# Pooled attention product on 64x64 tiles inside the value product, and a TensorE order that weighs changes of tile mode

## The chip, the core and the metric

The kernel runs on one core of a Trainium2 chip. Its engines work side by side, each on its own queue in program order: PE (TensorE, matrix products into PSUM), DVE (VectorE), ACT (ScalarE), POOL (GpSimd), and SP, which here only issues transfers (DMA). The metric is the device time of one execution in microseconds (us), as the median of several runs. PSUM has eight banks here: two for attention (`att`), one each for the gate and value products, and four for the output products (`o0` to `o3`).

## What is computed

The reference is attention followed by a gated layer. Attention is the sum of a local part (each query sees keys at most 3 positions away) and a pooled part (queries, keys and values averaged over groups of 4, full softmax over 144 groups, the result repeated 4 times):

```
q_d, k_d, v_d = means of q, k, v over groups of 4 positions       # S 576 -> 144
out_up    = repeat(softmax(q_d k_d^T / sqrt(D)) v_d, 4)
out_local = softmax(mask(|i-j| < 4, q k^T / sqrt(D))) v           # both softmaxes divide by sum + 1e-9
x   = (out_up + out_local), heads side by side                    # 4608 x 512
out = (sigmoid(x w_gate) * (x w_val)) w_out                       # 512 -> 1536 -> 512
```

There are 8 batches and 8 heads, with 64 numbers a head.

## The kernel before

**Units and chunks.** Attention is cut into 32 units (u = 0 to 31), each two heads of one batch. The gated layer ("MoE") is cut into 9 chunks of 512 tokens. Units 0 to 7 (`early`) feed chunks 0 and 1, units 8 to 31 (`later`) the rest. Chunks 0 and 1 are plain products with 12 + 12 + 12 groups (`pg` gate, `pv` value, `po` output, 12 matmuls of 512 columns each); from chunk 2 on there are 42 pairs of `bank` products (256 columns, line L832) and `obank` output products (L971) in a seven-product scheme.

**A unit's steps.** In the names of the code, with the engine: `s` (PE, local scores, 20 products on 64x64 tiles, the four corners of the array taken in turn), `st`/`mx`/`sm` (DVE), `sb`/`tm` (POOL), `ex` (ACT); `tt0`, `tt1` (PE, transposes into `at`, L446), `tc0`, `tc1` (ACT, copies out of PSUM); `sd` (PE, pooled scores, tiles of 64 rows), `dm` (DVE), `de` (ACT), `dn` (POOL, the softmax weights `ad`); `dt` (PE, six transposes into `adt`), `dc` (ACT copy); `va`, `vB` (POOL, pooled values `vdblk`: the two heads' 64x64 blocks on the diagonal of a 128x128 tile, zeros beside them); `do` (PE, tile `od`: three full-array products of 144 columns, L418); `oc` (ACT, `od` scaled by `sxb` and repeated four times); `x` (PE, local value product, 20 products on 64x64 tiles of 58 columns, L423, into two banks, one for each half of the queries); `xa0`, `xa1` (DVE, L595 and L1276: bank times `sxb` plus `od`, into the chunk's input). `fp32` products leave two records each in the trace.

**What sets the order.** Every step is an `op` with an engine, a planned duration, predecessors and the banks it needs. `order()` walks through planned time: for each free engine it takes the ready op with the earliest due time `late`, where `GOALS` and `PACE` set the due times. The result is a fixed order on each engine. On PE, whatever is ready among the next `PACE['ahead']` MoE products competes with the attention steps. The function `bank` inside `later` always takes one of the two `att` banks.

**Weights and the first chunk.** Until about 160 us the weights are loaded and split into two fp16 halves (L225 to L255, ACT and DVE), while units 0 to 7 and chunk 0 run. `pg0` needs the attention outputs of units 0 to 3 (`xl`, L1293, on POOL or DVE) and the first low half of w_gate (`lo`, L255).

**Transfers.** SP issues all of them in order: `load_qk`, `load_qkd`, `load_vd`, `vload`, and the weight pieces of the pairs (`fetch`, L814). An issue that waits holds all later ones.

Of the kernel before, what the change touches and what calls it, by code (L numbers as in the profile page):

```python
# [22 lines left out]
PACE = {'a0': -6.52, 'a': 6.04, 's0': 25.787, 'sp': 8.115, 'e': 2.605, 's': -0.706, 'sd': 0.86, 'tt': 13.445, 'dt': 12.18, 'do': 15.987, 'x': 16.17, 'b3': -1.06, 'b4': -2.399, 'b5': -4.037, 'b6': -0.29, 'b7': 3.324, 'extra': -0.177, 'ahead': 36}  # L23
GOALS = {'x0': 33.486, 'x0s': 7.26, 'pv': 73.942, 'pvs': 6.2, 'x1': 117.291, 'x1s': 28.832, 'po': 221.56, 'pos': 26.01, 'c1': 150.991}
INTURN = ("s", "sd", "tt0_", "tt1_", "dn", "dt", "vB", "do", "x")
# [10 lines left out]
HALF = NJ * R  # L36
TURNS = ((0, 3), (3, NJ))
# [38 lines left out]
def attention_moe(ctx, tc, qk, qkd, v, vd, wg, wv, wo, mask, out):  # L76
# [73 lines left out]
    vdblk = [zeroed(nc.gpsimd, [P, NKC, P], F32, f"vdblk{i}") for i in range(2)]  # L150
    ad = zeroed(nc.gpsimd, [QM, 2, NKC, 2, WIN], F32, "ad")
    vring = cp.tile([P, NVR, NBLK * D], F32, tag="vring", name="vring")

    def vturn(b):
        pt = ps_a.tile([P, 512], F32, tag="att", name=uniq("mxt"))
        nc.tensor.transpose(pt[:1, :P], vm[b, "m1"], ident)
        return pt
# [6 lines left out]
    def spread(row, n, pt=None):  # L164

        if pt is None:
            pt = ps_a.tile([P, 512], F32, tag="att", name=uniq("mxt"))
        nc.tensor.matmul(pt[:, 256 : 256 + n], row.to_broadcast([n, P]), ident[:n, :n], start=True, stop=True)
        return pt[:, 256 : 256 + n]
# [136 lines left out]
    svb = cp.tile([P, B], F32, tag="svb", name="svb")  # L306
    sxb = cp.tile([P, B], F32, tag="sxb", name="sxb")
# [25 lines left out]
    def vscale(b, got):  # L333
        pow2(pvb[:, b : b + 1], got)
        inv_scaled(svb[:, b : b + 1], pvb[:, b : b + 1], 2.0 * VUP)
        nc.vector.tensor_scalar(out=sxb[:, b : b + 1], in0=svb[:, b : b + 1], scalar1=XUP / VUP, scalar2=None, op0=ALU.mult)
# [118 lines left out]

    def spans(r, segs):

        t0, t1 = r * HALF, min(r * HALF + HALF, S)
        return [(c, o + max(i, t0) - i, max(i, t0), min(i + w, t1)) for c, o, i, w in segs if max(i, t0) < min(i + w, t1)]

# [5 lines left out]
    SAME = dict(s="s{}", pb="pb{}", sd="sd{}", vB="vB{}", tt0="tt0_{}", tt1="tt1_{}", dn1="dn{}", dt="dt{}", do="do{}", x="x{}", xa1="xa1{}", qk="qk{}", tc0="tc0_{}", oc="oc{}", mx="mx1_{}", sm="sm{}")  # L466

    def later(u):
        b, hp = divmod(u, NPAIR)
        s = st[u] = {}  # L470
        AD, VDB = ad, vdblk[u % 2]
# [10 lines left out]
        def bank(name):  # L482
            return ps_a.tile([P, 512], F32, tag="att", name=name)
# [16 lines left out]
        def scores():  # L500
            s["s"] = [bank(f"s_{u}_{par}") for par in range(2)]
# [15 lines left out]
        def const(k, c):  # L517
            nc.scalar.activation(s[k], s[k], AF.Copy, scale=c, bias=EPS * c)
# [4 lines left out]
        def pooled():  # L523
            s["d"] = [bank(f"sd_{u}_{h}") for h in range(2)]
# [16 lines left out]
        def dnorm(qb):  # L541
            own(ad, u)
            nc.gpsimd.tensor_tensor(  # L543
                out=AD[:, qb].rearrange("p c h k -> p h c k")[:, :, :, :KC],
# [4 lines left out]
        def turn(i):  # L549
            s["a", i] = bank(f"at_{u}_{i}")  # L550
# [7 lines left out]
        def dturn():  # L558
            mine(ad, u)
            pt = s["ta"] = bank(f"adt_{u}")  # L560
            for c in range(NKC):
                for qb in range(2):
                    nc.tensor.transpose(pt[:, c * SD + qb * QM : c * SD + (qb + 1) * QM],  # L563
                                        AD[:, qb, c].rearrange("p h k -> p (h k)"), ident[:QM, :QM])

        def dturned():
            s["adt"] = wk.tile([P, NKC, SD], F32, tag="adt", name=f"adt16_{u}", bufs=1)
            nc.scalar.copy(s["adt"], s["ta"][:, : NKC * SD].rearrange("p (c q) -> p c q", c=NKC))

        def vB():  # L570
            own(VDB, u)
            for ps in HALVES:
                nc.gpsimd.tensor_tensor(out=VDB[ps, :, ps], in0=y()[ps, :, 0], in1=y()[ps, :, 1], op=ALU.add)
# [4 lines left out]
        def dout():  # L578
            mine(VDB, u)
            pt = s["do"] = bank(f"od_{u}")  # L580
            for c in range(NKC):
                product(pt[:, :SD], [VDB[:, c]], [s["adt"][:, c]], c == 0, c == NKC - 1)

        def dcopy():
            s["od"] = wk.tile([P, S], F32, tag="od", name=f"od_{u}")
            nc.scalar.activation(s["od"].rearrange("p (g f) -> p g f", f=4), s["do"][:, :SD].unsqueeze(2).to_broadcast([P, SD, 4]),
                                 AF.Copy, scale=sxb[:, b : b + 1])

        def local():
            s["x"] = [bank(f"x_{u}_{r}") for r in range(2)]  # L590
            each(value_pairs(u, s["at"], s["x"]))

        def both(r):
            for c, o, a, e in spans(r, segs_of_batch(b)):
                nc.vector.scalar_tensor_tensor(  # L595
                    out=xf(c)[:, hp, o : o + e - a], in0=s["x"][r][:, a - r * HALF : e - r * HALF],
                    scalar=sxb[:, b : b + 1], in1=s["od"][:, a:e], op0=ALU.mult, op1=ALU.add)
# [15 lines left out]
        add("vB", "P", 1.15, vB, ["va", old("do", 2)])  # L613
        add("s", "E", 0.75, scores, ["qk", old("tt1", 3), old("s", 1)], ["st0", "st1"])
# [1134 lines left out]
```

## Time and profile before

| | us |
|---|---|
| median of 3 runs (965.03 to 966.88) | 966.24 |
| the profiled execution | 966.05 |
| its span, first to last instruction | 964.3 |
| PE busy in the span | 936.0 |
| DVE, ACT, POOL busy | 720.5, 629.3, 378.3 |

The page's second part cuts the span into 40 slices of 24.1 us and gives each engine's busy share in tenths. The chain of the page's fourth part is walked back from the last instruction; 84% of it is PE. A row of the PE timeline gives the start, the length until the last product has drained, and the number of records; products overlap, so what a group costs is the distance from its start to the next group's start, not the length in the second column.

### The profile page before, as it was taken

What the parts mean: (1) busy time and instruction counts of PE and PEld (TensorE: products, weight loads), DVE (VectorE), ACT (ScalarE), POOL (GpSimd) and SP (SyncE); (2) the same over time, 40 slices, a digit from 0 to 9 for tenths busy, and PEclk for the clock granted to TensorE, in tenths of its full rate; (3) what the DMA queues carried; (4) which work ended last, traced back from release to release, by engine and by line L of the source; (5) the groups of instructions that cost most, each with busy time, mean ns of one, the idle gap of its engine ahead of it and who ended that gap; (6) DMA issues with size and microseconds to landing.
All of it is one profiled execution on the core that took longest, in us unless ns stands there. A gap on an engine that the chain in (4) does not pass through costs nothing.

```text
span 964.3 us, 23935 instructions
## 1 busy us (share of the span) xinstructions
PE 936.0 (97%) x9535; PEld 716.0 (74%) x9535; DVE 720.5 (75%) x1350; ACT 629.3 (65%) x1602; POOL 378.3 (39%) x387
## 2 busy tenths in 40 slices
PE   7788999999999999999999999999999999999998
PEld 5644544455548777788888888888888888888885
DVE  6899999578888679876868677787876686556644
ACT  6897775455446766677866776777667666555551
POOL 2264323356447655454555463256342133000000
PEclk9898999999999999999999999999999999999999
DMA  9899988264536887887878867786655555656631
GB/s 331 283 322 281 310 319 266 86 192 170 215 130 213 269 288 245 250 278 266 297 257 275 292 234 251 245 284 234 218 194 189 206 211 197 220 202 218 230 132 44
DMA packets 75360, 225.22 MB, mean 234 GB/s; under 512 B 18672, under 2 KB 29936, under 8 KB 74992
## 3 DMA queue, kind: packets, MB, share of 16 engines
q1 hardware_dynamic: 75248, 223.69, 68.2%
q8 instruction: 75, 1.23, 0.5%
q14 instruction: 37, 0.30, 0.1%
HBM read 196.66 MB, written 27.00 MB: 232 GB/s over the span
## 4 chain that ended last, share of the span: by engine, by line
PE 84%; DVE 6%; issue 1%; ACT 1%; DMA 1%; DVEq 0%; ACTq 0%
PE bank L832 39%; PE obank L971 16%; PE po L418 9%; PE pg L418 5%; PE pv L418 5%; PE x L423 2%; PE od L418 2%; PE s L423 2%; PE sd L423 2%; PE at L446 1%; PE adt L563 1%; DMA arena<-in_wg_dram 1%; DVE arena L712 1%; DVE arena L233 0%; DVE arena L229 0%
## 5 line engine op out<-in xcount | busy, mean ns | idle before, releaser
L832 PE MATMUL bank<-arena,wv 128*128 128x256 f16 x1764 | 220.2, 273 | 0.0
L832 PE MATMUL bank<-arena,wg 128*128 128x256 f16 x1764 | 220.1, 273 | 0.0
L832 PEld LDWEIGHTS <-wg 128*128 128x128 f16 x1764 | 171.3, 98 | 25.1 <-issue 0.8
L832 PEld LDWEIGHTS <-wv 128*128 128x128 f16 x1764 | 170.9, 98 | 25.4 <-issue 1.0
L971 PE MATMUL obank<-wo,spare 128*128 128x256 f16 x1071 | 147.3, 273 | 1.7 <-ACT obank L997 1.4
L971 PEld LDWEIGHTS <-spare 128*128 128x128 f16 x1071 | 103.3, 98 | 15.7 <-issue 3.3
L929 DVE SCALAR_TENSOR_TENSOR wo<-wg,wo 128x512 f16<-128x512 f32 (+1 forms) x136 | 93.2, 700 | 20.6 <-ACT wo L926 20.0
L715 POOL TENSOR_TENSOR wg<-wg 128x256 f32<-128x256 f32 x52 | 41.9, 806 | 127.5 <-DVE wo L929 110.8
L926 ACT ACTIVATE wo<-wg 128x512 f16<-128x512 f32 (+1 forms) x136 | 76.7, 577 | 17.8 <-DVE wg L862 9.3
L418 PE MATMUL po<-spare,wo 128*128 128x512 f16 x324 | 79.8, 380 | 0.0
L881 ACT COPY bank<-wv 128x256 f32<-128x256 f32 x84 | 31.7, 378 | 68.8 <-DVE wg L879 53.2
L879 DVE TENSOR_TENSOR wg<-bank,wv 128x512 f32<-128x512 f32 x63 | 43.4, 690 | 38.5 <-PE bank L832 34.5
L874 ACT COPY wv<-bank 128x512 f32<-128x512 f32 x84 | 48.8, 581 | 33.6 <-PE bank L832 32.8
L418 PE MATMUL pg<-arena,wg 128*128 128x512 f16 x288 | 67.7, 384 | 3.1 <-DVE wg L255 2.1
L418 PEld LDWEIGHTS <-wo 128*128 128x128 f16 x432 | 40.4, 98 | 39.7 <-issue 1.3
L418 PE MATMUL pv<-arena,wv 128*128 128x512 f16 x288 | 66.2, 379 | 0.0
L971 PE MATMUL obank<-wo,wv 128*128 128x256 f16 x357 | 58.4, 273 | 0.0
L543 POOL TENSOR_TENSOR ad<-e,sme 72x288 f32<-72x288 f32 x48 | 36.2, 770 | 53.3 <-DVE sme L521 25.0
L418 PEld LDWEIGHTS <-wg 128*128 128x128 f16 x288 | 28.0, 99 | 36.3 <-DVE wg L255 3.4
L712 POOL TENSOR_TENSOR arena<-arena 128x512 f16<-128x512 f32 (+1 forms) x27 | 29.0, 1077 | 61.7 <-ACT arena L708 61.7
L862 DVE SCALAR_TENSOR_TENSOR wg<-wg,bank 128x512 f32<-128x512 f32 x42 | 28.8, 685 | 30.3 <-PE bank L832 29.9
L418 PEld LDWEIGHTS <-wv 128*128 128x128 f16 x288 | 27.3, 98 | 31.6 <-issue 0.4
(200 smaller groups left out, 1838.4 us busy)
## 6 DMA issues: line engine op xcount, KB each, us to landing
wg<-wg SPq DMA_DIRECT2D x42, 896.0 KB, 4.7
wv<-wv SPq DMA_DIRECT2D x42, 896.0 KB, 4.7
spare<-wo SPq DMA_DIRECT2D x51, 448.0 KB, 4.9
qk<-in_qk_dram SPq DMA_DIRECT2D x30, 610.0 KB, 5.3
qkd<-in_qkd_dram SPq DMA_DIRECT2D x29, 576.0 KB, 5.7
arena<-in_wo_dram SPq DMA_DIRECT2D x24, 512.0 KB, 5.0
vd<-in_vd_dram SPq DMA_DIRECT2D x29, 384.0 KB, 5.1
vring<-in_v_dram SPq DMA_DIRECT2D x64, 160.0 KB, 5.4
```

Of the source, the lines that this page charges most:

```text
L418: nc.tensor.matmul(o, w[a], x[c], start=first and i == 0, stop=last and i == len(pairs) - 1)
L423: nc.tensor.matmul(o, w, x, start=True, stop=True)
L543: nc.gpsimd.tensor_tensor(out=AD[:, qb].rearrange("p c h k -> p h c k")[:, :, :, :KC], in0=s["e"][:, qb].rearrange("p h (c k) -> p h c k", ...
L712: eng.tensor_tensor(out=lo, in0=src, in1=hi, op=ALU.subtract)
L715: eng.tensor_tensor(out=o, in0=x, in1=y, op=ALU.subtract)
L832: nc.tensor.matmul(o, w[:, a, k], x[:, xb, k, c], start=start and z == 0, stop=z == len(mms) - 1, skip_group_check=True)
L874: op(f"sa_{n}_{i}", "A", 0.58, lambda i=i: nc.scalar.copy(snap(i)[:, HC:], banks[i]), [g(0), p("ad"), p("se")] + (["w1"] if n == 0 else []))
L879: lambda i=i: nc.vector.tensor_tensor(out=vsum(n) if i else duo(n)[:, 1], in0=banks[i], in1=snap(i)[:, :CH], op=ALU.add),
L881: op(f"se_{n}_{i}", "A", 0.38, lambda i=i: nc.scalar.copy(banks[i][:, LEFT], snap(i)[:, CH:]), [f"ad_{n}_{i}"])
L926: nc.scalar.activation(g()[:, blocks, 0], src.rearrange("p (b t) -> p b t", t=HC), AF.Copy, scale=GSCALE)
L929: nc.vector.scalar_tensor_tensor(out=g()[:, blocks, 1], in0=src.rearrange("p (b t) -> p b t", t=HC), scalar=GSCALE, in1=g()[:, blocks, 0], ...
L971: nc.tensor.matmul(obank[M][:, half], w[:, wb, a], g[:, xb, x], start=start and z == 0, stop=z == 5, skip_group_check=True)
```

## The change

- **Pooled product in the value product.** `do` and `oc` go. Pooled values are kept as rows (`vdrow`: for each head 64x64 blocks, in both halves of the partitions). POOL writes one half of the partitions for each head, and two new transfers of 64 partitions x 192 numbers (`vC`, `pooled_rows`, on SP) copy each to the other half. The weights `ad` are laid out by quarters, so that the transposed `adt` serves 64-row tiles. `x` now begins with 12 products of 64x64 by 72 columns (`pooled_values`) into columns 296 to 367 of the same two banks, and then does its 20 value products. So `x` waits for `dc` and `vC` as well.
- **Scaling moved into the softmax.** The factor `sxb` goes from the outputs into the constants of the softmax (`rxb`, units 8 on) or to `xh`/`xl` (units 0 to 7).
- **After the product.** `oc0`, `oc1` (ACT) copy the 72 pooled columns of each bank four times over; `xa0`, `xa1` (DVE) add bank and copy, and wait for `oc1`. The `xl` step is on DVE alone.
- **Order.** PE's planner adds `SWITCH` for leaving and for entering a small-tile mode, and an op in the present mode gets its due time `PACE['join']` earlier. `GOALS` and `PACE` have new values.
- **Banks.** Attention banks go through the planner, and `o2`, `o3` may be taken by attention once chunk 2's output is out, until the last chunk's output needs them.

```diff
-PACE = {'a0': -6.52, ..., 'x': 16.17, ..., 'ahead': 36}
-GOALS = {'x0': 33.486, ..., 'po': 221.56, 'pos': 26.01, 'c1': 150.991}
+PACE = {'a0': -6.766, ..., 'x': 16.315, ..., 'join': 4.235, 'ahead': 38}
+GOALS = {'x0': 35.024, ..., 'po': 214.321, 'pos': 25.101, 'c1': 158.179}
+SWITCH = 0.11
...
-    vdblk = [zeroed(nc.gpsimd, [P, NKC, P], F32, f"vdblk{i}") for i in range(2)]
-    ad = zeroed(nc.gpsimd, [QM, 2, NKC, 2, WIN], F32, "ad")
+    vdrow = [zeroed(nc.gpsimd, [P, 2, NKC, D], F32, f"vdrow{i}") for i in range(2)]
+    ad = zeroed(nc.gpsimd, [QM, NKC, 2, 2, WIN], F32, "ad")
...
+    def pooled_values(u, adt, pts):
+        return [(pts[r][HALVES[h], DCOL : DCOL + QM], vdrow[u % 2][HALVES[r], h, c], adt[HALVES[r], c, h], c)
+                for c in range(NKC) for h in range(2) for r in range(2)]
+
+    def products(u, adt, at, pts):
+        for o, w, x, c in pooled_values(u, adt, pts):
+            nc.tensor.matmul(o, w, x, start=c == 0, stop=c == NKC - 1)
+        each(value_pairs(u, at, pts))
...
+    def four_times(s, u, r):
+        if r == 0:
+            s["od"] = wk.tile([P, S], F32, tag="od", name=f"od_{u}")
+        nc.scalar.copy(s["od"][:, 4 * QM * r : 4 * QM * (r + 1)].rearrange("p (g f) -> p g f", f=4),
+                       s["x"][r][:, DCOL : DCOL + QM].unsqueeze(2).to_broadcast([P, QM, 4]))
+
+    def add_pooled(s, out_, r, a, e):
+        nc.vector.tensor_tensor(out=out_, in0=s["x"][r][:, a - r * HALF : e - r * HALF], in1=s["od"][:, a:e], op=ALU.add)
+
+    def pooled_rows(u):
+        for h, ps in enumerate(HALVES):
+            nc.sync.dma_start(vdrow[u % 2][HALVES[1 - h], h], vdrow[u % 2][ps, h])
...
-        def bank(name):
-            return ps_a.tile([P, 512], F32, tag="att", name=name)
+        def held_bank(k, z, name):
+            return bank(f"{n(k)}.{z}", name)
...
-        add("vB", "P", 1.15, vB, ["va", old("do", 2)])
-        add("s", "E", 0.75, scores, ["qk", old("tt1", 3), old("s", 1)], ["st0", "st1"])
+        add("vB", "P", 1.3, vB, ["va", old("x", 2)])
+        add("vC", "D", 0.5, lambda: pooled_rows(u), ["vB"])
+        add("s", "E", 0.6, scores, ["qk", old("tt1", 3), old("s", 1)], ["st0", "st1"])
...
-        add("dc", "A", 0.52, dturned, ["dt", old("do", 1)])
-        add("do", "E", 0.76, dout, ["dc", "vB", f"vs_{b}!"], ["oc"])
-        add("oc", "A", 0.68, dcopy, ["do", old("xa1", 2), old("oc", 1), f"vs_{b}!"])
-        add("x", "E", 0.75, local, ["tc0", "tc1", "vw"], ["xa0", "xa1"])
+        add("dc", "A", 0.52, dturned, ["dt", old("x", 2)])
+        add("x", "E", 0.96, local, ["tc0", "tc1", "vw", "dc", "vC"], ["xa0", "xa1"])
+        for r in range(2):
+            add(f"oc{r}", "A", 0.46, lambda r=r: four_times(s, u, r), ["x", "oc0" if r else None, old("xa1", 2)])
...
-        unit_op("xl", "P", 1.6, xlow, ["xh"], use=["xs_"], alt=("V", 0.85))
+        unit_op("xl", "V", 0.9, xlow, ["xh"], use=["xs_"])
...
+        mode = lambda k: "" if ops[k]["eng"] != "E" else "sd" if k[:2] == "sd" else k[0] if k[0] in "sx" and k[1] in "_01234567" else ""
+        corner = {"s": 1, "x": 1, "sd": 2, "": 0}
...
-                choice = tag if type(tag) is list else [tag]
+                choice = [tag]
+                if type(tag) is list:
+                    choice = tag + ["o2", "o3"] * all(end.get(f"ev_2_{e}", 1e9) <= now for e in (2, 3))
...
+                        if at_:
+                            choices = sorted(choices, key=lambda z: z[0] - PACE["join"] * (corner[mode(z[1])] == at_))
...
+                    if x == "E":
+                        to = corner[mode(k)]
+                        end[k] += SWITCH * ((at_ > 0 and at_ != to) + (to > 0 and at_ != to))
+                        at_ = to
```

Three places in the engines' orders show what the diff alone does not.

PE, the pooled product of a later unit before. The wide rows beside it are MoE products; `vdblk` is the block-diagonal tile of pooled values.

```order
L832 LDWEIGHTS wv_115
L832 MATMUL bank_3495<-arena,wv_115 128x256
L418 MATMUL od_5680<-adt_18_5304,vdblk_117 128x144 x3
L971 LDWEIGHTS spare
L971 MATMUL obank_5501<-wo_116,spare 128x256
```

Now the pooled products open the `x` group (rows with `vdrow`, 64x72), here of a later unit that follows its MoE rows, and a group of its own is gone.

```order
L1000 LDWEIGHTS spare
L1000 MATMUL obank_5692<-wo_116,spare 128x256
L467 MATMUL x_0_5849<-adt_5601,vdrow_117 64x72
L467 MATMUL x_1_5850<-adt_5601,vdrow_117 64x72
L467 MATMUL x_0_5849<-adt_5601,vdrow_117 64x72
```

The end of an `x` group where the scores of another unit follow at once, with no MoE product between (nine such places from chunk 1 on: six `x` then `s`, three `s` then `x`; none before):

```order
L428 MATMUL x_1_6900<-at_6805,vring 64x58
L428 MATMUL x_0_6899<-at_6805,vring 64x58
L428 MATMUL x_1_6900<-at_6805,vring 64x58
L428 MATMUL s_0_6937<-qk_6413 64x64
L428 MATMUL s_1_6938<-qk_6413 64x64
```

From chunk 1's first gate product to the end, PE enters a small-tile mode 70 times before and 61 times now. All 72 `od` products of the 24 units there are gone.

SP, around chunk 1's output (stores are the rows with `out_dram`; the rows with `wv` and `wg` on the left are the pairs' weight pieces, `vring` the local values). Before:

```order
L401 DMA vd_3779<-in_vd_dram 128x768
L393 DMA qkd_3796<-in_qkd_dram 128x1152
L315 DMA vring<-in_v_dram 64x2x320 x2
L1108 DMA out_dram<-arena 128x1024
L814 DMA wg_114<-wg_140 128x3584
L401 DMA vd_3886<-in_vd_dram 128x768
```

Now:

```order
L841 DMA wg_114<-wg_145 128x3584
L318 DMA vring<-in_v_dram 64x2x320 x2
L486 DMA vdrow_117<-vdrow_117 64x192 x2
L406 DMA vd_4042<-in_vd_dram 128x768
L1137 DMA out_dram<-arena 128x1024
```

The two `vC` transfers of a unit stand ahead of the next unit's `vd` load, on the queue that also carries the pairs' weights.

DVE, where the first low halves of the weights are made (rows with `sw`); `spare` holds a unit's attention output, `arena` the chunk's input, `x` the value product's bank. Before:

```order
L276 TENSOR_SCALAR sw<-ew 128x4
L283 TENSOR_SCALAR tsc<-ew,pvb 128x2
L1179 TENSOR_TENSOR t_723<-s_0_721,mx_758 128x320
L1175 TENSOR_REDUCE mx_758<-s_1_722 128x5
L1179 TENSOR_TENSOR t_723<-s_1_722,mx_758 128x320
L229 TENSOR_SCALAR wg_114<-wg_114 128x512 x2
L255 SCALAR_TENSOR_TENSOR wg_114<-wg_114,sw 128x512
```

Now:

```order
L236 SCALAR_TENSOR_TENSOR wg_114<-arena,wg_114 128x512
L482 TENSOR_TENSOR spare<-x_0_864,od_911 128x290
L482 TENSOR_TENSOR spare<-x_1_865,od_911 128x286
L1235 TENSOR_REDUCE mxd_1_923<-sd_1_826 72x2
L1208 TENSOR_TENSOR t_770<-s_1_769,mx_800 128x320
L1298 SCALAR_TENSOR_TENSOR arena<-spare,sxb,arena 128x512
L1298 SCALAR_TENSOR_TENSOR arena<-spare,sxb,arena 128x64
L258 SCALAR_TENSOR_TENSOR wg_114<-wg_114,sw 128x512
```

The fourth unit's `xa` and `xl` now stand ahead of the first low half; before, they came after it (`xa` at rows 86 and 87, `xl` at 91 and 92, the first low half at 79; now 88, 89, 92, 93 and 94). The last low half of w_out stands at row 293 of DVE before and at 301 now.

## Rows read from the trace of the kernel before

**Rows 1.** The page: busy time and share, and PE in the 40 slices.
```profile
PE 936.0 (97%) x9535; PEld 716.0 (74%) x9535; DVE 720.5 (75%) x1350; ACT 629.3 (65%) x1602; POOL 378.3 (39%) x387
...
PE   7788999999999999999999999999999999999998
```

**Rows 2.** Windows: stretch, length, then busy us of each engine, clock, DMA.
```profile
0.00:165.00 165.00, 143.07 (x1314) 83.44 (x1315) 148.94 (x307) 122.29 (x308) 57.47 (x61) 0.94 0.91 306
165.00:300.00 135.00, 135.00 (x1157) 71.14 (x1155) 102.23 (x183) 69.81 (x177) 73.95 (x61) 1.00 0.46 156
300.00:770.00 470.00, 469.00 (x5402) 397.16 (x5392) 352.27 (x663) 334.30 (x890) 223.37 (x241) 1.00 0.74 251
770.00:964.30 194.30, 188.95 (x1681) 164.22 (x1679) 117.07 (x200) 102.88 (x227) 23.52 (x26) 1.00 0.53 183
```

**Rows 3.** PE timeline in the solid stretch: start, length, line, product, records.
```profile
414.62 1.47 PE L832 MATMUL bank<-arena,wv 128*128 128x256 f16 x12
416.02 0.81 PE L423 MATMUL s<-qk 64*64 64x64 f32 x40
416.77 1.48 PE L832 MATMUL bank<-arena,wg 128*128 128x256 f16 x12
418.09 0.90 PE L418 MATMUL od<-adt,vdblk 128*128 128x144 f32 x6
418.83 0.82 PE L832 MATMUL bank<-arena,wv 128*128 128x256 f16 x6
...
421.17 1.47 PE L832 MATMUL bank<-arena,wv 128*128 128x256 f16 x12
422.58 0.81 PE L423 MATMUL x<-at,vring 64*64 64x58 f32 x40
423.31 0.83 PE L832 MATMUL bank<-arena,wg 128*128 128x256 f16 x6
...
425.29 1.47 PE L832 MATMUL bank<-arena,wg 128*128 128x256 f16 x12
426.69 0.71 PE L423 MATMUL sd<-qks 64*72 64x144 f32 x8
427.34 0.28 PE L832 MATMUL bank<-arena,wv 128*128 128x256 f16 x1
```

**Rows 4.** PE timeline where scores and value product stand side by side.
```profile
22.32 0.81 PE L1170 MATMUL s<-wo 64*64 64x64 f32 x40 [0.35 <-DMA wo<-in_qk_dram]
22.95 0.79 PE L423 MATMUL x<-at,vring 64*64 64x58 f32 x40
23.67 0.50 PE L93 MATMUL awake<-idle 128*128 128x256 bf16 x3
```

**Rows 5.** Instructions by line: busy, mean ns, then idle before and releaser.
```profile
L586 ACT ACTIVATE od<-od,sxb 128x576 f32<-128x576 f32 x24 | 17.7, 739 | 6.2 <-PE od L418 5.8
L450 ACT COPY at<-at 128x348 f32<-128x348 f32 x32 | 14.4, 448 | 10.5 <-PE at L446 10.4
L997 ACT COPY obank<-wo 128x256 f32<-128x256 f32 x34 | 12.8, 376 | 10.7 <-DVE wo L996 10.6
L595 DVE SCALAR_TENSOR_TENSOR arena<-x,sxb,od 128x286 f32<-128x286 f32 x16 | 8.1, 504 | 1.1 <-PE x L423 0.9
L1179 DVE TENSOR_TENSOR t<-s,mx 128x320 f32<-128x320 f32 x16 | 7.7, 483 | 0.5
```

**Rows 6.** PE timeline: first gate product of chunk 0, and of chunk 1.
```profile
54.34 2.76 PE L418 MATMUL pg<-arena,wg 128*128 128x512 f16 x12
...
178.25 2.75 PE L418 MATMUL pg<-arena,wg 128*128 128x512 f16 x12
```

**Rows 7.** Windows, columns as in rows 2, between those two products.
```profile
54.34:178.25 123.91, 114.25 (x829) 57.74 (x825) 114.85 (x226) 89.00 (x210) 46.46 (x42) 0.97 0.85 283
```

**Rows 8.** Transfers: count, KB each, median us from issue to landing.
```profile
wo<-wo SPq DMA_DIRECT2D x36, 64.0 KB, 4.4
```

**Rows 9.** PE's waits over the span: releaser, us in total, times, longest.
```profile
PE s L423 <- ACT at L450: 1.5, 1, 1.5
```

More of the change, by code (lines that the diff above doesn't have):

```diff
@@ L334, in vscale @@
         pow2(pvb[:, b : b + 1], got)
-        inv_scaled(svb[:, b : b + 1], pvb[:, b : b + 1], 2.0 * VUP)
-        nc.vector.tensor_scalar(out=sxb[:, b : b + 1], in0=svb[:, b : b + 1], scalar1=XUP / VUP, scalar2=None, op0=ALU.mult)
+        if b < 2:
+            inv_scaled(sxb[:, b : b + 1], pvb[:, b : b + 1], 2.0 * XUP)
+        else:
+            nc.vector.tensor_scalar(out=rxb[:, b], in0=unit, scalar1=pvb[:, b : b + 1], scalar2=None, op0=ALU.mult)
     def batch_scales(b):
@@ L459, in spans, with pooled_turns, pooled_copy, quarter @@
         return [(c, o + max(i, t0) - i, max(i, t0), min(i + w, t1)) for c, o, i, w in segs if max(i, t0) < min(i + w, t1)]
+    def four_times(s, u, r):
[8 more added lines that the diff above has]
+            nc.sync.dma_start(vdrow[u % 2][HALVES[1 - h], h], vdrow[u % 2][ps, h])
+    def pooled_turns(pt, u):
+        mine(ad, u)
+        for c in range(NKC):
+            for h in range(2):
+                z = (2 * c + h) * QM
+                nc.tensor.transpose(pt[:, z : z + QM], ad[:, c, h].rearrange("p q k -> p (q k)"), ident[:QM, :QM])
+    def pooled_copy(u, pt):
+        adt = wk.tile([P, NKC, 2, QM], F32, tag="adt", name=f"adt_{u}", bufs=2)
+        nc.scalar.copy(adt, pt[:, : NKC * SD].rearrange("p (c h q) -> p c h q", c=NKC, h=2))
+        return adt
+    def quarter(qb):
+        return ad[:, :, :, qb, :KC].rearrange("p c h k -> p h c k")
     def pooled_pairs(s, pts):
@@ L470, in later @@
         s = st[u] = {}
-        AD, VDB = ad, vdblk[u % 2]
+        VDB = vdrow[u % 2]
         def n(k):
@@ L1231, in dturn @@
         def dturn():
-            pt = s["ta"] = bank(n("ta_"), f"adt_{u}")
-            s["adt"] = wk.tile([P, NKC, SD], F32, tag="adt", name=f"adt16_{u}", bufs=1)
-            for c in range(NKC):
-                for qb in range(2):
-                    nc.tensor.transpose(pt[:, c * SD + qb * QM : c * SD + (qb + 1) * QM],
-                                        AD[:, qb, c].rearrange("p h k -> p (h k)"), ident[:QM, :QM])
+            s["ta"] = bank(n("ta_"), f"adt_{u}")
+            own(ad, u)
+            pooled_turns(s["ta"], u)
         def dturned():
-            nc.scalar.copy(s["adt"], s["ta"][:, : NKC * SD].rearrange("p (c q) -> p c q", c=NKC))
+            s["adt"] = pooled_copy(u, s["ta"])
         def vdb():
@@ L1466, in attention_moe @@
                     tile_out(c, 2 * j + r, z % 4, k, first, last, [f"gl_{m}_{r}"] + (["wl"] if j0 else [])
+                             + ([f"xa{r_}_{u}" for u in range(NU - 8, NU) for r_ in range(2)] if j0 and first and z % 4 > 1 else [])
                              + (([f"ev_{c - 1}_{z % 4}"] if not j0 else [f"a{y}_{NSTR // 2 - 2}_{z % 4}" for y in range(2)] if z % 4 < 2 else []) if first else []))
```

157 lines of the change are left out of this document (64 added, 93 removed).

## The prediction

> **What bounds the kernel now.** I read the page first: PE is busy 97% of the span, DVE 75%, and PE's slices are below 9 tenths only in the first six of 40 [rows 1]. A busy PE in a pipelined engine proves little, so next come the windows by stage [rows 2]. From 165 to 300 us PE is busy 135.0 of 135 us, and from 300 to 770 us, where the later units run, 469 of 470, with DVE at 352, ACT at 334 and POOL at 223. PE waits there for almost nothing; of the list of waits the one row of scores that waited for a copy is 1.5 us, once [rows 9]. So from about 165 us on the time is the sum of what PE is given to do, and an attention step costs exactly the room that it takes in PE's row. In the first 165 us PE is busy only 143 us while DVE is busy 149 and the transfers 91%: that stage is not PE's alone, and PE's savings pass through only in part.
>
> Third, the PE timeline in the solid stretch gives that room. Twelve MoE products take 1.32 us from start to the next start (416.77 to 418.09). The pooled product `od` takes 418.09 to 418.83, 0.74 us, and starts with no gap. The scores take 416.02 to 416.77, 0.75 us, and start 416.02 - (414.62 + 1.32) = 0.08 us late; the value product 0.73 us and 0.09 late; the pooled scores 0.65 and 0.08 late [rows 3]. The start is late only for the three products on small tiles. I take 0.08 us as the price of entering that mode. Leaving it is hidden in the 0.75: where a value product follows scores directly, the same 40 records take 22.32 to 22.95, 0.63 us [rows 4], so leaving costs 0.12.
>
> **The change part by part.**
>
> *The pooled product leaves.* 24 units in the solid stretch, each 0.74 us: 24 x 0.74 = 17.8 us removed.
>
> *It comes back on four corners.* 12 products, so 24 records, of 72 columns inside `x`, no mode change of their own. No row shows this form. From above: the value product's 0.73 us for 40 records of 58 columns, scaled by records and columns, 0.73 x 24/40 x 72/58 = 0.54 us. From below: half of the tile in `od` is zeros, and the corners skip them; half of 0.74 is 0.37. Nearest is the undisturbed run of scores in [rows 4], 0.63 us for 40 records of 64 columns: 0.63 x 24/40 x 72/64 = 0.42 us, which I take, because that row has neither entry nor exit in it. 24 x 0.42 = 10.1 us added. Net of the two: 7.7 us, between 24 x 0.20 = 4.8 and 24 x 0.37 = 8.9.
>
> The value product shows 18 ns a record over its 0.73 us. TensorE: Matmul & The Clock Gate (the Trainium skill), section Back-to-back issue gap, speaks against this part: it gives products of 1 to 64 columns a floor of about 25 ns each, so that small ones gain nothing from being smaller. By that page, as an estimate, the pooled part would take 24 x 25 ns = 0.60 us and the solid stretch would save 24 x 0.14 + 1.8 = 5.2 us instead of 9.5; this trace disagrees, with 40 records in 0.73 us.
>
> *Fewer mode changes.* The order has 61 entries into a small-tile mode from chunk 1 on, before 70, since nine times scores and value product stand together. 9 x (0.08 + 0.12) = 1.8 us; at least 9 x 0.08 = 0.7.
>
> Sum for the solid stretch: 7.7 + 1.8 = 9.5 us, between 5.5 and 10.7.
>
> *ACT.* One `oc` of 739 ns becomes two copies of 288 columns out of PSUM. Copies of 256 and 348 columns take 376 and 448 ns [rows 5], so about 400 each: 0.06 us more a unit. ACT is idle 136 of 470 us [rows 2]; nothing on the path. *DVE.* `xa` changes from 504 ns to a plain addition out of PSUM; 320 columns of one take 483 [rows 5], so it is the same. `vscale` loses two tiny steps. *POOL* writes compact rows instead of a diagonal; it is busy 223 of 470. If that cover were gone (an engine in time with PE), each unit would pay these on the path: 0.06 for ACT, nothing for DVE.
>
> *The new transfers and waits.* `vC` waits on SP for POOL's `vB`; queued behind it are the next `vd` load and the pairs' weights. But the next `vd` load waits for the same `vB` already, since it overwrites its input, so the queue stops no later than before. `x` waits for the landing: small transfers of 64 KB land after 4.4 us [rows 8]. I counted for units 13 on what PE has to do, at the durations of [rows 3], between the release of the weight piece that stands ahead of `vC` on SP and that unit's `x`: at least 7.6 us, mostly 18 to 57. So nothing on the path there. In the first stage the fourth unit's `x` leads to the first gate product; one landing in full would cost 4.4 us once.
>
> *The first stage.* Between chunk 0's first gate product at 54.34 [rows 6] and chunk 1's at 178.25 there are 123.9 us in which PE is busy 114.25 [rows 7], so 9.7 us are lost. Four units lie in it; their pooled products free 4 x 0.32 = 1.3 us. DVE's rows up to the last low half of w_out are 301 for 293, but two long reductions go to POOL and `xl` of four units comes from there: the same work within about a microsecond. The order brings the fourth unit's `xl` ahead of the first low half, where both must be done before chunk 0 can go on, and so does not lengthen the chain. I take a gain of 2 us: the 1.3 and a little of the idle. Ends: a gain of 1.3 + 9.7 = 11 us if all idle time goes, a loss of 4.4 us for one landing on the chain.
>
> *Lent banks* cost nothing themselves: the output products that own `o2` and `o3` come back to them only with the last chunk, behind the last unit.
>
> Total: 9.5 + 2.0 = 11.5 us. The profiled execution took 966.05 us, 1.75 around its span of 964.3, and 0.19 below the median of 966.24; so 954.5 for a like execution and **954.7 us** for the median.
>
> **The rivals.** About 0.2% (1.9 us) is what a measurement of this kernel can tell from no change.
>
> *The first stage gives much more.* For: 9.7 us of PE time are lost there, and the order makes chunk 0's gate and value products wait for fewer rows of DVE. Against: DVE is busy 149 of 165 us, transfers 91%, and neither has less to do. All of it: 966.2 - 9.5 - 11 = 945.7 us; I give 945 to 950.
>
> *The corners are not cheap.* The upper bound of 0.54 us and no gain from leaving the mode: 5.5 us in the solid stretch and nothing before: 960.7, range 959 to 963. For: the value product's own row. Against: that row contains the exit. The page's floor named above comes out close by, at 966.2 - 5.2 = 961.0.
>
> *What is saved is lost again in the first stage.* Two landings of 4.4 us on the chain to the first gate product, 8.8 us, against 9.5 saved: 965.5, no change. For: transfers are 91% busy there. Against: units overlap, and only one stands last.
>
> *Slower: the banks.* Before, `oc` ran before `x`, and `x` gave its two banks back after two `xa`. Now both banks also wait for two copies on ACT, 2 x 0.40 = 0.8 us longer a unit, and until chunk 2's output is out there are only two banks. If PE had nothing else to do meanwhile, 24 x 0.8 = 19.2 us would come back: 966.2 - 11.5 + 19.2 = 973.9. It decides from (11.5 + 1.9)/24 = 0.56 us a unit on. TensorEngine Tiling (Array Packing) (the Trainium skill), section PSUM Bottleneck, warns of just this, that emptying PSUM becomes the limit after tiles have sped up TensorE. Against: PE waited once for such a copy [rows 9], MoE products stand between nearly all groups, and the joined ones come with lent banks.
>
> **How the numbers follow.** Forecast, 950 to 959 us: 0.58. First stage gives more: 0.12. Corners dear: 0.13. Lost again: 0.08, within 0.2%. Banks: 0.09, slower. So faster 0.58 + 0.12 + 0.13 = 0.83, same 0.08, slower 0.09. The range of 946 to 963 leaves out the last two and the lower tip of the second, 0.2 in all.
>
> **What would show it.** In the solid stretch an `x` group with its 64 records should take about 0.73 + 0.42 = 1.15 us to the next start, with no `od` rows; 0.54 more than 0.73 means dear corners. A joined pair should lack about 0.2 us. Chunk 1's first gate product should start near 176; earlier than 170 is the first rival, later than 181 the third. PE's busy time from 300 us to the last attention step should stay within 1% of the stretch; rows of PE waiting for `xa`, `oc` or `vdrow` that sum to over 5 us would be the last rival, and the forecast would be wrong.

## The result, and the profile after

The changed kernel takes 957.07 us (median of 4 runs, 955.06 to 957.83) against 965.63 for the kernel before in the same comparison (4 runs, 963.71 to 966.88): ratio 0.9897, 95% interval 0.9872 to 0.9921. Forecast were 954.7 us and a range of 946 to 963. The profiled execution took 955.06 us with a span of 953.3, 11.0 less than before; forecast were 11.5.

The page of the changed kernel (busy time, PE in 40 slices, the clock in tenths), then its windows with the columns of [rows 2]:

```profile
PE 925.7 (97%) x10130; PEld 705.9 (74%) x10130; DVE 721.2 (76%) x1341; ACT 636.5 (67%) x1630; POOL 378.4 (40%) x388
...
PE   7888999999999999999999999999999999999998
...
PEclk8898999999999999999999999999999999999999
```
```profile
300.00:770.00 470.00, 467.87 (x5824) 397.47 (x5822) 361.49 (x662) 344.78 (x922) 237.34 (x246) 1.00 0.77 262
770.00:953.30 183.30, 179.38 (x1597) 155.95 (x1594) 111.06 (x192) 96.84 (x214) 16.31 (x17) 1.00 0.52 182
```

PE is as full as in [rows 1, 2]. The last of these windows is 11.0 us shorter than that of [rows 2], so what was saved lies ahead of it. The first gate products of chunk 0 and chunk 1, as in [rows 6], and the window between them, as in [rows 7]:

```profile
55.24 2.99 PE L423 MATMUL pg<-arena,wg 128*128 128x512 f16 x12
...
178.65 2.76 PE L423 MATMUL pg<-arena,wg 128*128 128x512 f16 x12
```
```profile
55.24:178.65 123.41, 113.97 (x902) 55.73 (x897) 112.35 (x224) 89.41 (x201) 34.58 (x36) 0.96 0.87 284
```

Chunk 1 begins at 178.65 us; it was 178.25. From there to the end of the span it was 964.3 - 178.25 = 786.05 us and is 953.3 - 178.65 = 774.65. **By these two profiles the solid stretch gave 11.4 us, where 9.5 were forecast, and the first stage took 0.4, where a gain of 2.0 was forecast.** Below, "chunk 1" is the start of its first gate product, and "the rest" is from there to the end of the span. The profile after is a good execution, the fastest of its four: runs below with the same order ahead of chunk 1 show it between 178.65 and 181.1 us, and runs that change nothing behind it show a rest of 774.6 to 776.7. So the solid stretch gave 9.4 to 11.4 us, and the first stage lost 0.4 to 2.8, all against a single profile of the kernel before. The medians agree: a gain of 8.6 us, 2.9 short of the forecast.

The 0.4 us are the sum of two parts. Chunk 0's first gate product came 0.9 us later than before (55.24 for 54.34), and the distance from it to chunk 1 shrank by 0.5 (123.41 for 123.91). In the other three profiles with the same order and work up to chunk 1, chunk 0 begins at 55.67 to 56.96 us and the distance is 124.1 to 124.5. So the larger part of the spread of chunk 1's start comes from ahead of chunk 0.

The PE timeline of the solid stretch shows the new group, once behind scores and once ahead of them (start, length, line, product, records):

```profile
460.52 0.81 PE L428 MATMUL s<-qk 64*64 64x64 f32 x40
461.16 0.58 PE L467 MATMUL x<-adt,vdrow 64*64 64x72 f32 x24
461.53 0.78 PE L428 MATMUL x<-at,vring 64*64 64x58 f32 x40
462.25 1.48 PE L859 MATMUL bank<-arena,wg 128*128 128x256 f16 x12
...
505.84 0.61 PE L467 MATMUL x<-adt,vdrow 64*64 64x72 f32 x24
506.26 0.76 PE L428 MATMUL x<-at,vring 64*64 64x58 f32 x40
506.84 0.77 PE L428 MATMUL s<-qk 64*64 64x64 f32 x40
507.54 1.48 PE L859 MATMUL bank<-arena,wg 128*128 128x256 f16 x12
```

From start to next start the pooled part takes 0.42 us (505.84 to 506.26) and 0.37 behind scores; joined pairs take 1.73 and 1.70 us without their entry. The other units read alike: 0.42 to 0.43 alone, 0.37 to 0.38 joined, a value part of 0.69 to 0.72 us at a group's end and of 0.58 where scores follow.

PE's waits from chunk 1 to the end (releaser: us, times, longest), and ACT's new row in the form of [rows 5]:

```profile
PE bank L859 <- DVE wg L889: 1.4, 2, 0.9
PE po L423 <- DVE spare L1103: 0.5, 1, 0.5
PE obank L1000 <- ACT obank L1026: 0.2, 1, 0.2
```
```profile
L478 ACT COPY od<-x 128x288 f32<-128x288 f32 x64 | 22.8, 400 | 16.3 <-PE x L428 16.3
```

No product waits there for the copies `od`, for `xa` or for the new transfers, which land after 4.9 us (median of 64).

### The profile page after: what moved, and what is told of

The parts are those of the page before. It is cut to its first block, busy times and chain, and to the rows that moved or that the text cites. A ratio compares the mean times of both kernels' runs of the same rounds, so it can differ in the third digit from the quotient of the medians.

```text
span 953.3 us, 25222 instructions
## 1 busy us (share of the span) xinstructions
PE 925.7 (97%) x10130; PEld 705.9 (74%) x10130; DVE 721.2 (76%) x1341; ACT 636.5 (67%) x1630; POOL 378.4 (40%) x388
## 4 chain that ended last, share of the span: by engine, by line
PE 87%; DVE 6%; DMA 4%; ACT 1%; issue 1%; SPq 1%; POOL 0%; DVEq 0%; POOLq 0%
PE bank L859 39%; PE obank L1000 16%; PE po L423 10%; PE pg L423 6%; PE pv L423 6%; PE sd L428 2%; PE x L428 2%; PE s L428 2%; DMA vring<-in_v_dram 2%; PE x L467 2%; PE at L451 1%; DMA wv<-in_vd_dram 1%; PE adt L493 1%; DMA arena<-in_wg_dram 1%; DVE wo L958 1%
## 5 line engine op out<-in xcount | busy, mean ns | idle before, releaser
L958 DVE SCALAR_TENSOR_TENSOR wo<-wg,wo 128x512 f16<-128x512 f32 (+1 forms) x136 | 96.4, 725 | 16.3 <-ACT wo L955 16.2
L955 ACT ACTIVATE wo<-wg 128x512 f16<-128x512 f32 (+1 forms) x136 | 76.4, 576 | 17.5 <-DVE wg L889 9.8
L739 POOL TENSOR_TENSOR arena<-arena 128x512 f16<-128x512 f32 (+1 forms) x23 | 24.7, 1081 | 58.6 <-ACT arena L735 58.6
```

What stands on the lines that cost most here:

```text
L955: nc.scalar.activation(g()[:, blocks, 0], src.rearrange("p (b t) -> p b t", t=HC), AF.Copy, scale=GSCALE)
L958: nc.vector.scalar_tensor_tensor(out=g()[:, blocks, 1], in0=src.rearrange("p (b t) -> p b t", t=HC), scalar=GSCALE, in1=g()[:, blocks, 0], ...
```

## The experiments

Each edit is made in the changed kernel. Chunk 1 and the rest are from one profile a kernel, with the spreads named above (2.5 and 2 us); whole times are medians, and ratios are to the kernel before.

### The corners and the joins in the solid stretch

```diff
-        for o, w, x, c in pooled_values(u, adt, pts):
-            nc.tensor.matmul(...)
+        for z in range(2 if u >= NPLAIN else 1):
+            for o, w, x, c in pooled_values(u, adt, pts):
+                nc.tensor.matmul(...)
```


> The 12 pooled products of units 8 to 31 are done twice (the second writes the same numbers again). Theory (these units lie where PE alone sets the time, 0.43 us a pass): 24 x 0.43 = 10.3 us more, 967.4 us, chunk 1's start unchanged. Rival (PE has room there after all): less than 3 us more.

966.85 us, ratio 1.0014 (0.9995 to 1.0032). The rest took 784.0 us, 9.4 more than after the change (7.3 at least, by the spread), so a second pass of one unit costs 9.4/24 = 0.39 us (0.30 at least). The rows say 0.37: 48 records take 0.80 us up to the value part, where 24 took 0.43. The price of the corners is real time on PE and not a reading of overlapping rows.

```diff
-                    choice = tag + ["o2", "o3"] * all(...)
+                    choice = tag
```


> The changed kernel without the two lent output banks; the planner still counts changes of tile mode. Its order has no joined pair either from chunk 1 on (70 entries into a small-tile mode for 61), and up to chunk 1 it is the same order. Theory (banks matter only through the nine joins): chunk 1 starts at the same 178.6 us, from there on 2.2 us more, 959.3 us. Rival (two banks are too few now that a unit's value product holds both through two copies): PE waits for xa or for the copies, some 0.2 to 0.8 us a unit, 5 to 19 us more, 962 to 976 us.

962.25 us, ratio 0.9964 (0.9944 to 0.9984). Without the lent banks the order has 70 entries into small-tile modes again and no joined pairs. The rest took 778.0 us, 3.4 more; PE's idle time there grew by 1.1, which leaves 2.3 for nine entries: about 0.25 each, where 0.20 had been put. PE's busy time there grew by the same 2.3 us, and none of its waits is for `xa` or a copy, so the rival of too few banks does not show. The whole time is 5.2 us above the changed kernel's and not 2.2: 3.4 of it in the rest, and the remainder in a first stage of the same order, within its spread.

```diff
-'join': 4.235
+'join': 0.0
-SWITCH = 0.11
+SWITCH = 0.0
```


> The changed kernel with SWITCH and PACE['join'] at 0, so that PE's planner no longer weighs changes of tile mode; corners, lent banks and goals stay. In its order no scores stand beside a value product from chunk 1 on (before this edit nine times). Theory (from chunk 1 on the time is the sum of what PE is given, and a joined pair saves about 0.25 us, as the changed kernel's timeline shows): the stretch from chunk 1's first gate product to the end grows by 9 x 0.25 = 2.2 us, to about 959.3 us in all if the first stage stays. Rival (the joins are worth nothing, the gain is the corners' alone): that stretch stays within 0.5 us, 957 us.

968.66 us, ratio 1.0019 (0.9997 to 1.0042): nearly all of the gain is gone, and neither expectation held. The rest took 779.7 us, 5.0 more. Of this 4.0 are more idle time of PE, eight more entries (69 for 61) make 2.0 at 0.25 each, 12 MoE products that now stand ahead of chunk 1 take 2.6 away, and 1.6 are open. But chunk 1 itself came at 189.6, 11 us later, in an execution that is the slowest of its ten; by the medians (11.6 us in all) the first stage has about 6.6 of it. The rule on modes changes the order of the first stage too, and that was the larger part.

### The banks and the new transfers

```diff
+        for z in range(2 if u >= NPLAIN else 1):
             nc.scalar.copy(s["od"][...], ...)
```


> The copies oc0 and oc1 of units 8 to 31 are each done twice on ACT (the second writes the same numbers), which holds a value product's banks about 0.8 us longer a unit. Theory (PE has MoE products to do meanwhile, ACT has room): no change, 957 us within 1.5. Rival (the banks are held to the limit): up to 24 x 0.8 = 19 us more, 976 us.

958.38 us, ratio 0.9919 (0.9897 to 0.9940), the rest 775.1 (0.4 more). Each copy doubled, which adds 15.4 us to ACT's busy time in the rest, 0.64 a unit before the banks come free, is hardly seen on PE. For the order of the changed kernel the last rival of the prediction is out. TensorEngine Tiling (Array Packing) (the Trainium skill), section PSUM Bottleneck, warns that copies out of PSUM may become the limit; by this run's 0.4 us they have not.

```diff
     def pooled_rows(u):
-        for h, ps in enumerate(HALVES):
-            nc.sync.dma_start(...)
+        return
```


> Leaves out vC, the two small transfers of each unit that copy the compact rows to the other half of the partitions (the corners multiply zeros there). Theory V (the transfers and SP's wait in them took the first stage's gain): chunk 1's first gate product 2 to 5 us earlier, near 176, whole time near 954. Rival (they stand on no chain): chunk 1 within the 2.5 us in which kernels of the same first-stage order differ (178.7 to 181.1), whole time within 1 us of the changed kernel's 957. From chunk 1 on both expect 774.7 within 1.

958.77 us, ratio 0.9917 (0.9898 to 0.9936); chunk 1 at 181.5. Without the new transfers nothing is won, so they did not take the first stage's gain. The rest took 777.1 us, a little beyond the spread, with 2.2 us more of idle time of PE, spread over several waits; why is open.

### What sets the first stage

Three runs add work there, one each to DVE, to the transfers and to PE.

```diff
     def wlow(k, i):
+        for z in range(2 if k == "o" else 1):
             nc.vector.scalar_tensor_tensor(out=lo, ...)
```


> The low halves of w_out's 12 pieces are made twice on DVE (same numbers), 12 x 0.77 = 9.2 us more of DVE at the end of the first stage. Theory A (VectorE's chain to the last weight sets chunk 1's start): chunk 1 starts 6 to 9 us later and the time is 963 to 966 us. Theory B (transfers set it): within 2 us, 957 to 959 us.

965.34 us, ratio 0.9983 (0.9971 to 0.9996), chunk 1 at 188.1, 9.4 later. DVE's busy time between the two gate products grew by 7.9 us (112.35 to 120.22), and the distance between them is 132.75 us, 8.3 to 9.3 more than in the four profiles without the extra work: DVE's work counts in full.

```diff
+        for z in range(2 if k == "o" and n else 1):
             nc.sync.dma_start(t..., srcs[k][i]...)
```


> The 12 loads of w_out's pieces that feed the split are issued twice (same bytes to the same place), 6.3 MB more, about 20 us at the 302 GB/s of the first 165 us. Theory B (transfers set chunk 1's start): 8 to 20 us later, 965 to 977 us. Theory A (VectorE sets it, the transfers have room): within 3 us, up to 960 us.

994.47 us, ratio 1.0287 (1.0263 to 1.0311), chunk 1 at 218.0, 39 later. This is far above the bytes, since each second load waits on SP until the first has landed in the same tile. SP's waits from 55 to 218 us:

```profile
SPq L222 <- DMA arena<-in_wo_dram: 53.9, 12, 6.0
```

So it shows that waiting transfers count, and nothing on bandwidth.

```diff
+        for z in range(2 if u < NPLAIN else 1):
             for o, w, x, c in pooled_values(u, adt, pts): ...
```


> The 12 pooled products of units 0 to 7 are done twice, those of the later units once. Theory (before chunk 1 PE's work is hidden behind transfers and VectorE, so the pooled product's saving in the early units gave nothing): chunk 1 starts within 1 us of 178.6 and the time stays at 957 to 958 us. Rival (PE sets that stage too): 8 x 0.43 = 3.4 us more, chunk 1 at 182.1, 960.5 us.

961.36 us, ratio 0.9948 (0.9929 to 0.9968): 4.3 us more for 8 x 0.43 = 3.4 us of PE's work. My theory that early work of PE is hidden fell. In the profile, the slowest of the four executions, chunk 1 is even 7.9 us later, and two groups of twelve MoE products that take 2.59 us from start to start elsewhere are stretched to 3.91 and 5.10:

```profile
89.34 4.07 PE L423 MATMUL pv<-arena,wv 128*128 128x512 f16 x12
120.13 5.30 PE L423 MATMUL pg<-arena,wg 128*128 128x512 f16 x12
```

In the changed kernel the same two take 3.62 and 3.91 us. So 1.5 us of the delay in this profile are slower products and not added ones, and the 4.3 us need not be the added work alone.

Two runs then take work away.

```diff
     def wlow(k, i):
+        if k == "o":
+            nc.vector.memset(lo, 0.0)
+            return
```


> Leaves out the low half of w_out's split: DVE's 12 subtractions of 0.744 us before chunk 1 become 12 fills with zero (estimated 0.2 us each from the fills in the trace), so DVE has about 6.5 us less to do before chunk 1, the reverse of the run that did them twice. Theory A (DVE's order sets chunk 1's start and nothing stands close behind it): chunk 1's first gate product 5 to 6.5 us earlier than with the changed kernel, near 174, whole time near 951. Rival (DVE, transfers and PE stand in turn, each right behind the other; adding to one costs in full, taking from one gives little): chunk 1 at most 2 us earlier, 955 to 957. From chunk 1 on both expect the 774.7 us of the changed kernel, within 1.5.

957.50 us, ratio 0.9903 (0.9881 to 0.9926). A fill takes 0.272 us. DVE's busy time between the two gate products fell by 5.5 us (112.35 to 106.88), and chunk 1 came at 181.4, no earlier; the distance between them is 124.6 us, no shorter. (The 0.744 us of the expectation are rows of w_gate; those of w_out take 0.93.) Theory A holds for added work only. The timeline of PE shows a cause that I had not put up:

```profile
113.82 0.52 PE L454 MATMUL at<-ident,t 128*128 128x128 f32 x3 [0.59 <-ACT adt L500]
...
115.85 0.27 PE L267 MATMUL mxt<-ident,vm 128*1 128x128 f32 x1 [1.20 <-ACT at L458]
...
116.63 0.58 PE L275 MATMUL mxt<-ident,mxr 1*128 1x1 f32 x2 [0.29 <-DVE mxr L271]
117.15 5.30 PE L426 MATMUL pg<-arena,wg 128*128 128x512 f16 x12
```

After 2.1 us of gaps (0.59, 1.20, 0.29) between small products the gate products take 5.1 us to the next start instead of 2.59, at a granted clock of 0.50. In the changed kernel they take 3.91, so the further 1.2 us hide a part of what the shorter work of DVE could give, and not all 5.5.

```diff
+        last = 0 if u < 8 else NKC - 1
-        for o, w, x, c in pooled_values(u, adt, pts):
+        for o, w, x, c in pooled_values(u, adt, pts)[: 4 * (last + 1)]:
...
```


> Leaves out two of the three key blocks of the pooled product in units 0 to 7 (8 records instead of 24), all of them before chunk 1: 8 x 0.28 = 2.2 us of PE's work less there, the reverse of the run that did them twice. Theory P (PE's work in the first stage counts in full, as the added 3.4 us cost 4.3): whole time 2 to 3 us below the changed kernel, near 954.5. Rival (taken from PE there it is lost to the other chains, as the forecast gain was): within 1 us of 957. From chunk 1 on both expect 774.7 within 1.

957.17 us, ratio 0.9905 (0.9884 to 0.9925), chunk 1 at 179.7: the whole time shows nothing. Only half of the 2.2 us lies between the two gate products, and the distance there is 122.7 us, 0.7 to 1.8 below the four profiles with the full work. So the saving may have come through; this run alone says little.

### The order of before for the new work

```diff
-PACE = {...}   # the change's values
-GOALS = {...}
+PACE = {...}   # the values of before, with 'join': 4.235
+GOALS = {...}
```


> The changed kernel with GOALS and PACE of the kernel before (PACE['join'] kept). Its order has 65 entries into a small-tile mode from chunk 1 on and five joined pairs instead of nine. Theory (goals matter for the joins and hardly for the first stage): 4 x 0.25 = 1 us more from chunk 1 on, chunk 1 within 1.5 us of 178.6, 958 us. Rival (the new goals hold back a first stage that would have gained): chunk 1 starts at 176 or earlier and the time is 955 us or less. Other rival (the new goals are what made the gain): chunk 1 starts 4 us later or more, 962 us.

975.52 us, ratio 1.0096 (1.0066 to 1.0126): slower than before. Chunk 1 came at 182.7, and the rest took 795.1, 20.5 more. Ahead of chunk 1 stand 96 of chunk 0's output products instead of 132, so 36 more of 0.216 us, 7.8 us, follow behind it; four more entries are 1.0 us; 5.8 us are more waits of PE; and the clock fell once in the solid stretch. Timeline of PE and windows (stretch, length, PE, PEld, DVE, ACT, POOL, clock, DMA):

```profile
318.56 0.43 PE L428 MATMUL sd<-qks 64*72 64x144 f32 x2 [1.89 <-DVE arena L482]
319.43 1.23 PE L428 MATMUL sd<-qks 64*72 64x144 f32 x6 [0.44 <-DVE arena L482]
320.59 2.74 PE L859 MATMUL bank<-arena,wg 128*128 128x256 f16 x12
323.13 2.77 PE L859 MATMUL bank<-arena,wv 128*128 128x256 f16 x12
325.69 1.52 PE L859 MATMUL bank<-arena,wg 128*128 128x256 f16 x12
```
```profile
318.50:322.00 3.50, 3.00 (x15) 2.03 (x16) 3.15 (x6) 2.96 (x6) 1.19 (x2) 0.57 0.01 5
322.00:326.00 4.00, 4.00 (x22) 2.87 (x21) 2.31 (x3) 2.63 (x12) 0.74 (x1) 0.53 0.38 56
```

Waits of 1.89 and 0.44 us for DVE's `xa` are followed by 7.5 us with a mean granted clock of 0.53 to 0.57, so nearly all at the level of 1.2 GHz, in which 24 products take 5.10 us (320.59 to 325.69) and not 2 x 1.31. As an estimate from the two windows that dip costs 3.5 x 0.43 + 4.0 x 0.47 = 3.4 us beside the 2.3 of the waits. The remaining 2.5 us of the 20.5 are not settled. With these due times PE does wait for `xa`, so the run on copies above speaks for the changed kernel's order alone.

### The clock in the first stage

In the changed kernel's own trace the same thing stands in two places between the two gate products. PE's timeline at the second of them, after and, below it, before:

```profile
111.67 0.52 PE L451 MATMUL at<-ident,t 128*128 128x128 f32 x3 [0.59 <-ACT adt L497]
112.12 0.38 PE L272 MATMUL mxt<-ident,mxr 8*128 8x8 f32 x2
113.52 0.27 PE L264 MATMUL mxt<-ident,vm 128*1 128x128 f32 x1 [1.02 <-ACT at L455]
...
114.48 0.58 PE L272 MATMUL mxt<-ident,mxr 1*128 1x1 f32 x2 [0.47 <-DVE mxr L268]
114.99 4.07 PE L423 MATMUL pg<-arena,wg 128*128 128x512 f16 x12
118.90 2.75 PE L423 MATMUL pv<-arena,wv 128*128 128x512 f16 x12
```
```profile
113.11 0.32 PE L423 MATMUL s<-qk 64*64 64x64 f32 x2 [1.51 <-ACT at L450]
113.91 0.81 PE L423 MATMUL s<-qk 64*64 64x64 f32 x38 [0.48 <-DVE spare L1276]
114.65 0.27 PE L261 MATMUL mxt<-ident,hmx 128*8 128x128 f32 x1
114.85 0.71 PE L423 MATMUL sd<-qks 64*72 64x144 f32 x8
115.50 0.59 PE L1236 MATMUL adt<-ident,ad 72*128 72x72 f32 x6
115.93 2.75 PE L418 MATMUL pv<-arena,wv 128*128 128x512 f16 x12
```

Both kernels have gaps of about 2 us here. Before, longer groups stood around them, and the value products ran at the full clock (1.00 from 115.93 to 118.61 us); after, the order leaves only transposes and tiny products, and the gate products take 3.91 us, 1.3 too many, at a granted clock of 0.66. The other place, near 80 us, has the half clock in both kernels. Before:

```profile
81.97 0.38 PE L269 MATMUL mxt<-ident,mxr 8*128 8x8 f32 x2
82.28 0.76 PE L446 MATMUL at<-ident,t 128*128 128x128 f32 x5
84.81 0.33 PE L1166 MATMUL s<-arena,eye 64*64 64x320 bf16 x4 [1.76 <-ACT at L450]
84.94 1.22 PE L1170 MATMUL s<-qk 64*64 64x64 f32 x40
...
89.48 3.94 PE L418 MATMUL pg<-arena,wg 128*128 128x512 f16 x12
```

There the granted clock is 1.00 up to 84.94 us and 0.51 from there to 89.48, behind a gap of 1.76 us that has only transposes and tiny products just ahead of it, and the gate products take 3.79 us.

The kernel already has products of zeros that nobody reads (`awake`, rows L93 and L95), but its planner puts them only ahead of chunk 0's first gate product. The last run fills the gaps at both places:

```diff
+        fill = {"wg4p": 5, "tt0_4": 13, "tt0_5": 5, "vs1p": 9, "vs1r": 4}
         for k in seq:
             ...
+            if k in fill:
+                awake(fill[k], "gate")
             ops[k]["f"]()
```


> Puts 36 products of zeros that nobody reads (0.11 us each) into five gaps of PE in the first stage of the changed kernel: 18 into 79 to 81.5 us, 18 into 111 to 114.5 us. After these gaps the changed kernel's trace shows the clock at half: the forty score products at 83.66 take 1.21 us to the next start instead of 0.75, the twelve value products at 84.87 3.62 and the twelve gate products at 114.99 3.91 instead of 2.60, in all 2.8 us; before the change the second of these places ran at the full clock. Theory C (the lost clock took the first stage's gain): those groups at 0.75, 2.60 and 2.60 us, chunk 1's first gate product 2 to 3 us earlier, 175.5 to 177, whole time near 954.5. Rival (three chains stand in turn, as in the runs that took work from DVE, from SP and from PE): the clock comes back there, but chunk 1 stays at 178.7 to 181.5 and the whole time within 1.2 us of 957. From chunk 1 on both expect 774.7 within 1.

**952.77 us** (951.55 to 953.58, 6 runs), ratio 0.9849 (0.9820 to 0.9878). Theory C holds, and the time is 1.7 us below what it put. The second place and chunk 1 in its timeline, and both places as windows, of the changed kernel and then with the fill:

```profile
110.66 1.16 PE L95 MATMUL awake<-idle 128*128 128x256 bf16 x9
...
112.32 0.60 PE L95 MATMUL awake<-idle 128*128 128x256 bf16 x4
...
113.34 2.76 PE L423 MATMUL pg<-arena,wg 128*128 128x512 f16 x12
...
175.69 2.76 PE L423 MATMUL pg<-arena,wg 128*128 128x512 f16 x12
```
```profile
78.50:91.10 12.60, 10.53 (x84) 5.78 (x84) 10.56 (x24) 10.41 (x25) 4.14 (x4) 0.73 1.01 283
110.40:121.50 11.10, 9.02 (x43) 4.45 (x42) 9.78 (x25) 8.52 (x17) 0.83 (x1) 0.85 0.92 314
```
```profile
78.50:91.10 12.60, 12.35 (x115) 7.13 (x112) 11.61 (x26) 11.29 (x28) 4.65 (x5) 1.00 1.01 289
110.40:121.50 11.10, 10.81 (x59) 5.67 (x59) 10.89 (x26) 7.98 (x16) 0.00 (x0) 1.00 0.94 324
```

The clock is 1.00 at both places, and chunk 1 comes at 175.69 us, 3.0 earlier; the rest took 775.8. The distance from chunk 0 to chunk 1 is 120.3 us, 3.2 less than in the changed kernel's profile, so the 2.8 us of slow products came through in full. Four us of added products made the kernel 4.3 us faster by the medians. All its executions are below all of the changed kernel's (955.06 to 957.83), but the two stand in different comparisons: the kernel before had 968.46 us beside this one. By the ratios, which take that out, the intervals still touch (0.9878 and 0.9872).

The kernel before's own executions show one reason why they are wide. Of its eleven executions beside this run four took 963.67 to 964.40 us at a mean granted clock of 0.991 to 0.992, and seven 968.34 to 970.07 at 0.984 to 0.986. The changed kernel's four executions had 0.984 to 0.986, the filled one's six 0.989 to 0.994. Set beside the executions of before at a like clock, the changed kernel is 12 us faster and the filled one 11, close to the 11.5 of the forecast. This is read from the record, across comparisons, and no run tests it; the kernel before was not filled, so what of the 952.77 us it could have had too is not known.

## Why the prediction was right, and where it was not

- **The bound.** Right. From chunk 1 on PE's waits sum to 2.3 us before and 2.1 after, and what was taken from PE there came out of the time. (One reading was off: in [rows 1] PE's slices are below 9 tenths in the first four and the last, not in the first six.)
- **The corners at 0.42 us.** Right: 0.42 alone, 0.37 joined, 0.37 for the second pass when doubled. A unit's two products fall from 0.74 + 0.73 us to 1.12, so 24 of them give 8.4 us where 7.7 were put; the value part, at the end of a group, takes 0.69 and not 0.73. The dear corners are out. The floor of about 25 ns that TensorE: Matmul & The Clock Gate (the Trainium skill), section Back-to-back issue gap, gives for products of 1 to 64 columns is not seen: the value product's 40 records of 58 columns take 0.58 us where scores follow, 14.5 ns each. The pooled products, which the prediction priced by that floor too, have 72 columns and lie outside it; their 24 records in 0.42 us are 17.5 ns each.
- **Nine entries at 0.20 us.** Right in kind; 0.25 each by the run without lent banks, so 2.3 us for 1.8. With the corners this makes 10.7 us, within the 9.4 to 11.4 and at the upper end of the 5.5 to 10.7 that the prediction gave.
- **Other engines, transfers and banks at nothing.** Right in the solid stretch, for the changed kernel's order. The copies doubled cost 0.4 us, and leaving the transfers out won nothing; so the rival of two landings is out as well, though the run without lent banks, at 181.09 us, just met its sign.
- **The first stage.** Wrong, by 2.4 us in these profiles (up to 4.8 by the spread) and in sign. The step that failed is "the 1.3 and a little of the idle": it priced PE's gaps as lost time only and took the speed of the products behind them as given. The new order put two groups of transposes and three tiny products around the gaps at 111 to 115 us, and the twelve gate products behind them lost 1.3 us to the half clock. Filling that place and the one at 80 us, which both kernels have, brought chunk 1 to 175.69, by chance where the forecast had put it. In these two profiles the 1.3 us and the 0.9 by which chunk 0 itself began later make 2.2 of the 2.4; the prediction's sum had no term for the 0.9, and whether it is order or spread is open.
- **The total.** That 957.07 us lies within 2.4 of the forecast is in part luck: in these profiles the solid stretch gave more than its 9.5 and the first stage less than its 2.0.
- **What the prediction left out.** It gave the new `GOALS` and `PACE` no price. With the values of before the same products make the kernel slower than before, so the gain needs the retuned due times as much as the cheaper products. The kernel before with the new values was not run, so what the new due times would give there is not known; the rows of the corners and the entries account for the solid stretch without them.
- **"Does not lengthen the chain".** Not shown, and doubtful: chunk 0's first gate product stands at 54.34 us before and at 55.24 to 57.49 in the eight profiles with the changed order and work up to it (55.59 without the new transfers, so they are not the reason). There is one profile of before and no run that moves `xl` alone, so the cause is open. The runs show that the first stage has no single chain: work added to DVE counts in full, work added to PE shows too, and work taken from DVE alone gave nothing.

## To carry to other kernels

Where a PE timeline is gapless, an edit is worth the sum of its start-to-start distances, and rows of the old kernel give new small-tile products to a few hundredths of a microsecond. Where it has gaps, price what stands behind them as well: read the granted clock and the start-to-start time of the first large group, and try a few products that nobody reads in the gap before looking for a shorter chain. When the planner's due times are retuned along with an edit, run the edit with the old ones before giving the edit the credit.

## What was not expected of the hardware

- Gaps of 1.89 and 0.44 us close together, in a stretch where PE was otherwise full, were followed by 7.5 us at nearly half clock (0.53 to 0.57): the estimated loss behind the gaps (3.4 us) was larger than the gaps.
- Gaps of the same total, about 2 us, brought the half clock where only transposes and tiny products stood between them, and not where forty score products and eight pooled ones did. That is seen at one place each. In the other place of before a single gap of 1.76 us, behind transposes and tiny products, was enough. What decides it is not shown; the last run shows that with the gaps filled the clock stays at 1.00 at both places.
- The second pass of a corner product, with the array already in that mode, costs 0.37 us for 24 records of 72 columns.
